# Output gates of an mLSTM cell as half of 1 + tanh(o/2), one block at a time, on one Trainium2 core

## The chip, the core and the metric

The kernel runs on one core of a Trainium2 chip. The core has five engines with an instruction queue each: TensorE (PE) for matmuls and transposes, VectorE (DVE) and ScalarE (ACT) for elementwise work, GpSimd (POOL), and SyncE (SP), which here only issues DMAs. Each engine works strictly in the order of its own queue, and waits for another engine or for a DMA by a semaphore. The metric is device time in microseconds (us); lower is better.

## What is computed

Two blocks, the second fed by the first.

The mLSTM cell has 4 batches, 8 heads, 768 positions and a head size of 40. For every position t (shortened from the reference):

```python
m_new  = max(f_gate[t] + m, i_gate[t])
f_stab = exp(f_gate[t] + m - m_new);  i_stab = exp(i_gate[t] - m_new)
C = f_stab * C + i_stab * outer(v[t], k[t])
n = f_stab * n + i_stab * k[t]
h_tilde = C @ q[t]
denom = max(abs(n . q[t]), 1)
o = 1 / (1 + exp(-o_gate[t]))          # the output gate
y[t] = o * h_tilde / denom
```

The result becomes 3072 rows of 320 numbers. Hash routing sends every row to one of 8 experts, `token_ids * 2654435761 % 8`, which is `token_ids % 8`; an expert is two matmuls, 320 to 1024 with a ReLU, and 1024 to 320. All data is float32.

## The kernel before, in words

**The two stages.** The first stage works in the chunked form of the cell: a block is 128 positions of one batch, all 8 heads. There are 24 blocks, and the loop `for s in range(NT)` handles one per step, batch by batch within a chunk of positions, so that the state of a batch is used again four steps later. The finished rows `x` go to a DRAM tensor, `x_rows`. The second stage gathers the rows of each expert from there by indirect DMAs (`gather`, line 109) and runs the experts one after the other.

**The order of the work** is written out by hand (`manual_schedule`): what a step calls, in which order, is the order on each engine's queue. For a step s this is, with the lines of the profile:

- SP: loads of the gate rows `R` for step s+3 (line 210), of k and q for s+5 and v for s+4 (199), of the output gates `og` (195), then the stores of finished rows (457), then pieces of the first expert's weights (130 to 136).
- `divided(s-1)` on DVE (446 to 450): the division of block s-1, which reads the PSUM tile `xh` of that block and writes `x`.
- `turn(s+2)`: transposes of k and q on PE (332), copied out of PSUM (333), as a rule by ACT.
- pieces of the routing, a few small DVE and POOL operations each, listed by step in `pieces`. `route_hot(0..7)` builds one-hot matrices for 3 blocks each (DVE 614 and 622, POOL 619); every second one is followed at the end of its step by `route_table` (PE 630, then DVE 633 and 635). `route_index` makes the row lists (DVE 640 to 653), `route_tiles` the list of extra tiles (DVE 554 to 562).
- `scores(s+1)` on PE (379), `k_weights(s+1)` on POOL (365), `decays(s+1)`: PE 343, two `exp` on ACT (347), PE 351, then `qs` on DVE (355) and `dec` on ACT (357).
- `gated(i)` on POOL (454): x times the output gate.
- `state(s)`: PE 410 into the PSUM tile `xh` of the next block, a copy `add` on ACT (414), two additions on POOL (420). There is none from step 20 on.
- `weigh(s+1)` on DVE (385), then `attend(s)` on PE (431, 437).

At step 21 the first two gathers of expert 0 are issued on POOL; they read the rows of blocks 0 to 19, so they wait for those stores. At steps 22 and 23 their results are transposed on PE (`early_turn`, 675), ahead of `attend(23)`.

**The output gates before.** They are loaded in three groups of 8 blocks into a tile of 2560 elements per partition (2 buffers), from step 3 to 6, 7 to 11 and 13 to 16. One sigmoid (371) works on a whole group, at the end of steps 7, 12 and 17. The sigmoid and the `exp` of `decays` need different function tables, so a table load stands before each sigmoid and another before the next `exp`. In the step after a sigmoid the two copies of `turn` go to DVE and no block is gated. In the others up to two blocks a step are gated, from step 9 on; the gating stands ahead of `state(s)` on POOL's queue. `x` has 10 buffers, as blocks wait for their gates.

Of the kernel before, what the change touches and what calls it, by code (L numbers as in the profile page):

```python
# [17 lines left out]
P = 128  # L18
# [4 lines left out]
def kernel(  # L23
# [127 lines left out]
    with tc.tile_pool(name="gates", bufs=1) as gp, \  # L151
# [6 lines left out]
        NG, KV, RB = 8, 6, 3  # L158
# [26 lines left out]
        def rows_of(src, s):  # L185
            b, c = place(s)
            return src[b, :, c * P : (c + 1) * P, :].rearrange("h p d -> p h d")

        def load(s, what, eng=None):
            d = st.setdefault(s, {})  # L190
            eng = eng or nc.sync
            if what == "o":
                if s % NG == 0:
                    og[s // NG] = ld.tile([P, NG, H, D], F32, name="og", bufs=2)
                eng.dma_start(og[s // NG][:, s % NG], rows_of(o_gate, s))
            else:
                bufs, src = {"k": (ks, k), "q": (qs, q), "v": (vs, v)}[what]
                d[what] = bufs[s % KV]
                eng.dma_start(d[what][:, :, :D], rows_of(src, s))
# [127 lines left out]
        def turn(s, what, on_act=True):  # L327
            d = st[s]
            d[what + "T"] = wk.tile([P, PR, P], F32, name=what + "T", bufs=3)
            tp = ps.tile([P, PR, P], F32, name="tr", tag="tr", bufs=2)  # L330
            for j in range(PR):
                nc.tensor.transpose(tp[:, j, :], d[what][:, 2 * j : 2 * j + 2, :].rearrange("p h d -> p (h d)"), ident[:])  # L332
            (nc.scalar.copy if on_act else nc.vector.tensor_copy)(d[what + "T"][:], tp[:])
# [36 lines left out]
        def sigmoid(g):  # L370
            nc.scalar.activation(og[g][:], og[g][:], AF.Sigmoid)  # L371
# [70 lines left out]
        def divided(s):  # L442
# [6 lines left out]
            d["x"] = wk.tile([P, H, D], F32, name="x", bufs=10)  # L449
            nc.vector.tensor_tensor(d["x"][:], hs[:, :, :D], den[:].to_broadcast([P, H, D]), op=ALU.mult)  # L450

        def gated(s):
            x = st[s]["x"]
            nc.gpsimd.tensor_tensor(x[:], x[:], og[s // NG][:, s % NG], op=ALU.mult)  # L454
# [182 lines left out]
        def route_index():  # L637
# [20 lines left out]
            21: [route_index], 22: [route_tiles],  # L658
        }
        products = {4: [route_turned], 5: [route_counts]}  # L660
        for i, j in enumerate((11, 12, 14, 15, 16, 17, 19, 20)):
            pieces.setdefault(j, []).append(lambda i=i: route_hot(i))
            if i % 2:
                products[j] = [lambda i=i // 2: route_table(i)]
        for i, part in enumerate(slices_of(0)):
            pieces.setdefault((17, 18, 19, 20, 21, 22, 23)[i], []).append(part)
        sig_at = {7: 0, 12: 1, 17: 2}
        o_at = {}
        for i, j in enumerate((3, 3, 4, 4, 5, 5, 6, 6, 7, 8, 8, 9, 9, 10, 10, 11, 13, 13, 14, 14, 15, 15, 16, 16)):
            o_at.setdefault(j, []).append(i)  # L670
# [60 lines left out]
        nsig, ndone, waiting = -1, 0, {}  # L731
        for s in range(NT):
# [15 lines left out]
            for i in o_at.get(s, ()):  # L748
                load(i, "o")
# [10 lines left out]
            if s + 2 < NT:  # L760
                if s > 0:
                    turn(s + 2, "k", s - 1 not in sig_at)
                    turn(s + 2, "q", s - 1 not in sig_at)
# [14 lines left out]
            for i in range(2):  # L778
                if ndone < s and ndone // NG <= nsig and s - 1 not in sig_at:
                    gated(ndone)  # L780
                    waiting.setdefault(s + 1, []).append(ndone)
                    ndone += 1
# [11 lines left out]
            if s in sig_at:  # L794
                nsig = sig_at[s]
                sigmoid(nsig)
# [24 lines left out]
        while ndone < NT:  # L821
            gated(ndone)
            waiting.setdefault(NT, []).append(ndone)
            ndone += 1
# [202 lines left out]
```

## Time and profile before

| | |
|---|---|
| median of 5 runs | 386.65 us (386.06 to 387.17) |
| the profiled execution: its time, its span | 387.15 us, 385.3 us |
| busy share of the span, PE / DVE / ACT / POOL | 95% / 35% / 29% / 37% |
| first stage, up to the first expert matmul (873) | 136.24 us |
| 20 to 120 us: ACT busy / DVE busy / POOL busy | 63.6 / 78.2 / 67.7 us of 100 |

The span runs from the program's first instruction to its last. Busy time is the time in which an engine worked on an instruction; PE's matmuls are pipelined, so its own share is not a share of its peak. In a timeline row the columns are start (us), duration (us), engine, line, operation, what it writes and reads, shapes, count, and in brackets the idle time just before it with the instruction that ended it. Rows of one kind that follow closely are merged (x2, x16). The PSUM tile written by PE 332 at the head of a step marks its start; such starts give the length of each step.

### The profile page before, as it was taken

The numbers are of one execution on the slowest core, as the hardware profiler recorded it, in microseconds if no ns is written. First come the engines' busy times: TensorE is split into PE (matmuls) and PEld (weight loads), VectorE is DVE, ScalarE is ACT, GpSimd is POOL, SyncE is SP. The second block draws the span as 40 slices with busy tenths as digits, with TensorE's granted clock in tenths as the row PEclk, the third lists the DMA queues.
The fourth block names the chain that finished last, engine by engine and source line by source line (L and its number), as shares of the span: only waits on it lengthen the run. The fifth ranks groups of instructions, "written<-read, shape, count | busy, mean of one in ns | idle before, by whom it ended". The sixth has DMA issues, their size and how long they took to land.

```text
span 385.3 us, 7944 instructions
## 1 busy us (share of the span) xinstructions
PE 366.9 (95%) x3213; PEld 256.2 (66%) x3213; DVE 136.2 (35%) x354; ACT 112.8 (29%) x232; POOL 142.3 (37%) x243
## 2 busy tenths in 40 slices
PE   8989999899999889999999999999999999999991
PEld 8778788788878766865655655565665665664560
DVE  7568686988878821212012012002102102101100
ACT  6565576485585311111011111111111111101100
POOL 8433466889977417240141150124023020020121
PEclk9999999999999999999999999999999999999998
DMA  7699999998998599281721720442362000000000
GB/s 149 118 169 167 181 163 179 217 182 168 189 252 215 171 302 351 97 284 57 256 94 43 260 97 19 153 161 66 109 199 68 1 34 17 0 35 18 0 27 25
DMA packets 123797, 51.02 MB, mean 132 GB/s; under 512 B 103723, under 2 KB 119751, under 8 KB 123759
## 3 DMA queue, kind: packets, MB, share of 16 engines
q1 hardware_dynamic: 116254, 36.73, 41.1%
q0 software_dynamic: 2496, 8.20, 6.5%
q10 hardware_dynamic: 5008, 5.57, 4.7%
q8 instruction: 26, 0.43, 0.5%
q14 instruction: 13, 0.10, 0.1%
HBM read 42.10 MB, written 8.71 MB: 132 GB/s over the span
## 4 chain that ended last, share of the span: by engine, by line
PE 65%; DVE 7%; DMA 7%; POOL 6%; issue 6%; ACT 5%; SPq 2%; POOLq 0%; ACTq 0%; DVEq 0%
PE zp L902 22%; PE mh L873 22%; PE mh L866 6%; DMA x_rows<-x 4%; PE tr L332 2%; PE sp L379 2%; POOL x L454 2%; DVE w L385 2%; PE un L681 2%; ACT og L371 2%; DMA xr<-x_rows,g_idx 2%; PE xh L437 2%; PE tp L849 1%; PE zp L943 1%; PE ab L343 1%
## 5 line engine op out<-in xcount | busy, mean ns | idle before, releaser
L902 PE MATMUL zp<-w2t,h 128*128 128x320 f32 x384 | 105.5, 433 | 0.0
L873 PE MATMUL mh<-xT,w1t 128*128 128x416 f32 (+2 forms) x288 | 97.0, 481 | 1.3 <-DVE x L450 1.3
L902 PEld LDWEIGHTS zp<-w2t,h 128*128 128x128 f32 x384 | 72.6, 190 | 31.5 <-issue 2.9
L873 PEld LDWEIGHTS mh<-xT,w1t 128*128 128x128 f32 x288 | 51.3, 190 | 39.8 <-issue 37.8
L836 POOL DMA_INDIRECT out_dram<-zo,s_idx x26 | 25.7, 989 | 88.6 <-ACT zo L835 88.3
L855 DVE COPY xT<-tp 128x384 f32<-128x384 f32 x15 | 8.4, 557 | 127.9 <-PE tp L851 127.9
L882 ACT ACTIVATE h<-mh 128x416 f32<-128x416 f32 (+2 forms) x36 | 17.2, 479 | 110.0 <-PE mh L866 59.4
L835 ACT COPY zo<-zp 128x320 f32<-128x320 f32 x26 | 11.1, 426 | 101.4 <-PE zp L902 93.1
L880 DVE TENSOR_SCALAR h<-mh 128x416 f32<-128x416 f32 (+2 forms) x36 | 19.5, 543 | 59.2 <-PE mh L866 31.5
L437 PE MATMUL xh<-v,w 128*64 128x41 f32 x768 | 34.6, 222 | 0.0
L385 DVE TENSOR_TENSOR w<-sp,w 128x512 f32<-128x512 f32 x48 | 30.8, 681 | 8.5 <-ACT w L347 8.5
L379 PE MATMUL sp<-qT,kT 64*128 64x128 f32 x384 | 29.7, 285 | 2.4 <-DVE w L385 2.1
L347 ACT ACTIVATE w<-ab 128x512 f32<-128x512 f32 x48 | 26.1, 596 | 17.0 <-PE ab L343 17.0
L974 POOL COPY hrem<-h 128x256 f32<-128x256 f32 x8 | 3.2, 400 | 74.3 <-ACT h L882 74.3
L437 PEld LDWEIGHTS xh<-v,w 128*64 128x64 f32 x768 | 30.6, 138 | 0.0
L109 POOL DMA_INDIRECT xg<-x_rows,g_idx x24 | 23.4, 974 | 15.9 <-PE mh L866 6.9
L379 PEld LDWEIGHTS sp<-qT,kT 64*128 64x128 f32 x384 | 24.6, 187 | 7.0 <-issue 2.8
L866 PE MATMUL mh<-xT,w1c 64*128 64x416 f32 (+2 forms) x144 | 27.9, 497 | 0.1
L431 PE MATMUL xh<-C,qs 128*64 128x82 f32 x320 | 27.3, 249 | 0.0
L420 POOL TENSOR_TENSOR C<-C,add 64x164 f32<-64x164 f32 x32 | 17.8, 557 | 17.3 <-ACT add L414 16.1
L454 POOL TENSOR_TENSOR x<-x,og 128x320 f32<-128x320 f32 x24 | 20.5, 871 | 6.7 <-DVE x L450 6.6
L365 POOL TENSOR_TENSOR kw<-k,kwT 128x320 f32<-128x320 f32 x20 | 14.4, 724 | 12.5 <-PE xh L410 8.2
(187 smaller groups left out, 385.9 us busy)
## 6 DMA issues: line engine op xcount, KB each, us to landing
w2t<-in_moe_w_dram SPq DMA_DIRECT2D x5, 1280.0 KB
w1t<-in_moe_w_dram SPq DMA_DIRECT2D x5, 1024.0 KB
k<-in_k_dram SPq DMA_DIRECT2D x24, 160.0 KB
v<-in_v_dram SPq DMA_DIRECT2D x24, 160.0 KB
og<-in_o_gate_dram SPq DMA_DIRECT2D x24, 160.0 KB
x_rows<-x SPq DMA_DIRECT2D x24, 160.0 KB
q<-in_q_dram SPq DMA_DIRECT2D x23, 160.0 KB
w2t<-in_moe_w_dram ACTq DMA_DIRECT2D x2, 1280.0 KB
```

The lines of the kernel that those rows point to most:

```text
L109: nc.gpsimd.indirect_dma_start(out=xg, out_offset=None, in_=x_d[:rows, :], in_offset=bass.IndirectOffsetOnAxis(ap=idx, axis=0),)
L347: nc.scalar.activation(w[:, hf], ab[:], AF.Exp)
L379: nc.tensor.matmul(sp[hf][:, j, :], lhsT=d["kT"][r, j, :], rhs=d["qT"][r, j, :], start=True, stop=True)
L385: nc.vector.tensor_tensor(d["w"][:, hf], d["sp"][hf][:], d["w"][:, hf], op=ALU.mult)
L431: nc.tensor.matmul(xh[t, 2 * j : 2 * j + 2, :], lhsT=d["qs"][:, j, t], rhs=Cs[b][c % 2][:, j].rearrange("p h d -> p (h d)"), start=True, s ...
L437: nc.tensor.matmul(hs[t, 2 * j + hf, :], lhsT=d["w"][:, hf, j, t], rhs=d["v"][:, 2 * j + hf, :], start=(c == 0), stop=True, skip_group_che ...
L454: nc.gpsimd.tensor_tensor(x[:], x[:], og[s // NG][:, s % NG], op=ALU.mult)
L836: ins = nc.gpsimd.indirect_dma_start(out=out[:, :], out_offset=bass.IndirectOffsetOnAxis(ap=idx, axis=0), in_=zo[:], in_offset=None, bound ...
L866: nc.tensor.matmul(hp[i][:, : c1 - c0], lhsT=w1c[r, fp, :], rhs=xT[r, 2, c0:c1], start=first, stop=not first,)
L873: nc.tensor.matmul(hp[i][:, : c1 - c0], lhsT=w1t[:, db, fb * P : (fb + 1) * P], rhs=xT[:, db, c0:c1], start=(first and db == 0), stop=(not ...
L880: nc.vector.tensor_relu(h[:, 2 * fp, c0:c1], hp[i][:, : c1 - c0])
L902: nc.tensor.matmul(zp[:], lhsT=h[:, fb, j * P : (j + 1) * P], rhs=w[2][:, fb, :], start=(fb == 0), stop=(fb == FB - 1),)
```

## The change

- Each block's output gates have their own tile of 320 elements per partition, 6 buffers. They are loaded two steps ahead of their use (at step 21 for step 23), after v's load in SP's queue as before.
- The gate is computed by two ACT operations on that tile: `tanh(o/2)`, then half of it plus 0.5. They stand after `state(s)`, ahead of `attend(s)`. In the built order of the changed kernel the only table load on ACT is the very first one.
- Blocks 0 to 7 get their gates at steps 4, 5, 5, 6, 7, 7, 8, 9, and block i from 8 on at step i+1, but 22 and 23 both at step 23. A block is gated on POOL right after its gate, so after `state(s)` and not ahead of it, and stored at the next step: the first store is at step 5 instead of 10.
- All copies of `turn` are on ACT. `x` has 8 buffers.
- `route_hot` runs at steps 11 to 18 (before: 11, 12, 14, 15, 16, 17, 19, 20), the tables at 12, 14, 16, 18 (before 12, 15, 17, 20), `route_index` at 20 (21), `route_tiles` at 21 (22).

```diff
@@ def load
-                if s % NG == 0:
-                    og[s // NG] = ld.tile([P, NG, H, D], F32, name="og", bufs=2)
-                eng.dma_start(og[s // NG][:, s % NG], rows_of(o_gate, s))
+                og[s] = ld.tile([P, H, D], F32, name="og", bufs=6)
+                eng.dma_start(og[s][:], rows_of(o_gate, s))
@@ def turn
-            (nc.scalar.copy if on_act else nc.vector.tensor_copy)(d[what + "T"][:], tp[:])
+            nc.scalar.copy(d[what + "T"][:], tp[:])
@@
-        def sigmoid(g):
-            nc.scalar.activation(og[g][:], og[g][:], AF.Sigmoid)
+        def gate(s):
+            nc.scalar.activation(og[s][:], og[s][:], AF.Tanh, scale=0.5)
+            nc.scalar.activation(og[s][:], og[s][:], AF.Copy, scale=0.5, bias=0.5)
@@ def divided
-            d["x"] = wk.tile([P, H, D], F32, name="x", bufs=10)
+            d["x"] = wk.tile([P, H, D], F32, name="x", bufs=8)
@@ def gated
-            nc.gpsimd.tensor_tensor(x[:], x[:], og[s // NG][:, s % NG], op=ALU.mult)
+            nc.gpsimd.tensor_tensor(x[:], x[:], og.pop(s)[:], op=ALU.mult)
@@ the plan by steps
-            21: [route_index], 22: [route_tiles],
+            20: [route_index], 21: [route_tiles],
-        for i, j in enumerate((11, 12, 14, 15, 16, 17, 19, 20)):
-            pieces.setdefault(j, []).append(lambda i=i: route_hot(i))
+        for i in range(8):
+            pieces.setdefault(11 + i, []).append(lambda i=i: route_hot(i))
             if i % 2:
-                products[j] = [lambda i=i // 2: route_table(i)]
+                products[11 + i] = [lambda i=i // 2: route_table(i)]
-        sig_at = {7: 0, 12: 1, 17: 2}
-        o_at = {}
-        for i, j in enumerate((3, 3, 4, 4, 5, 5, 6, 6, 7, 8, 8, 9, 9, 10, 10, 11, 13, 13, 14, 14, 15, 15, 16, 16)):
-            o_at.setdefault(j, []).append(i)
+        gates_of = {}
+        for i, j in enumerate((4, 5, 5, 6, 7, 7, 8, 9)):
+            gates_of.setdefault(j, []).append(i)
+        for i in range(8, NT):
+            gates_of.setdefault(min(i + 1, NT - 1), []).append(i)
@@ the loop
-            for i in o_at.get(s, ()):
+            for i in gates_of.get(s + 2, ()) if s + 2 < NT - 1 else gates_of[NT - 1] if s == NT - 3 else ():
                 load(i, "o")
...
-                    turn(s + 2, "k", s - 1 not in sig_at)
-                    turn(s + 2, "q", s - 1 not in sig_at)
+                    turn(s + 2, "k")
+                    turn(s + 2, "q")
...
-            for i in range(2):
-                if ndone < s and ndone // NG <= nsig and s - 1 not in sig_at:
-                    gated(ndone)
-                    waiting.setdefault(s + 1, []).append(ndone)
-                    ndone += 1
             state(s)
...
-            if s in sig_at:
-                nsig = sig_at[s]
-                sigmoid(nsig)
+            for i in gates_of.get(s, ()):
+                gate(i)
+                if i < s:
+                    gated(i)
+                    waiting.setdefault(s + 1, []).append(i)
             if s == NT - 1:
                 early_turn(1)
             attend(s)
```

## The prediction

> **What bounds the kernel now.** I read the page's slices first, then PE's waits in the first stage, then the timeline step by step. From 136 us on PE works without a break on the experts and the change touches nothing there: what it is worth is decided before 136 us.
>
> ```profile
> PE   8989999899999889999999999999999999999991
> ...
> DMA  7699999998998599281721720442362000000000
> ```
>
> One slice is 9.6 us. PE is near full in the first 14 slices too, and so are the DMA queues; ACT is busy 63.6 of the 100 us from 20 to 120. So I measure steps by PE's starts of the k transposes: steps 7 and 8 take 4.83 us each (49.36, 54.19, 59.02), with no gap; a `route_table` adds 0.27 on PE, and 0.25 in the next step, where the q transposes wait for the copy out of PSUM. 4.83 plus these is the floor, and gains can come only from steps above it. PE's waits from 16 to 136 us (total us, times, longest) name them:
>
> ```profile
> PE xh L410 <- POOL C L390: 1.3, 1, 1.3
> PE sp L379 <- DVE w L385: 1.3, 2, 0.9
> PE tr L332 <- ACT dec L357: 0.9, 2, 0.4
> PE tr L332 <- ACT kT L333: 0.7, 1, 0.7
> ...
> PE tk L630 <- POOL oh_c L619: 0.2, 1, 0.2
> ```
>
> The two waits for `dec` belong to sigmoids. ACT's groups (count, busy us, mean ns) give the durations:
>
> ```profile
> L835 ACT COPY zo<-zp 128x320 f32<-128x320 f32 x26 | 11.1, 426 | 101.4 <-PE zp L902 93.1 <-PE zp L943 8.2
> L371 ACT ACTIVATE og<-og 128x2560 f32<-128x2560 f32 x3 | 7.0, 2339 | 0.0
> ...
> L371 ACT ACT_TABLE_LOAD x3 | 3.8, 1283 | 1.0 <-DMA x_rows<-x 1.0
> L347 ACT ACT_TABLE_LOAD x3 | 3.8, 1283 | 0.1
> ```
>
> **Part 1, the sigmoids go.** Each holds ACT for 1.28 + 2.34 + 1.28 = 4.9 us, 14.7 in all. What PE loses is in the rows after the first and the third:
>
> ```profile
> 60.10 0.66 PE L332 MATMUL tr<-ident,q 128*128 128x128 f32 x4 [0.43 <-ACT dec L357]
> ...
> 112.83 0.66 PE L332 MATMUL tr<-ident,q 128*128 128x128 f32 x4 [0.44 <-ACT dec L357]
> ```
>
> Step 9 runs from 59.02 to 64.68, 5.66 us, and step 19 from 111.74 to 117.41, 5.67: 0.83 and 0.84 over 4.83, the wait and the slower matmuls after it. The second sigmoid costs nothing: step 13 is 5.11 = 4.83 + 0.25 and step 14 is 4.83. Gain 1.67. The Trainium skill, "ScalarE: Activation LUTs", section "What ACT_TABLE_LOAD costs", counts about 2.66 us for a switch, a load of 1283 ns and a drain of 1380. The load agrees to the nanosecond, but here the `exp` starts at 111.64, 0.01 us after its load ended: no drain is paid, and by the rule the same sum would credit 16 us of ACT time instead of 7.7, still only as PE sees it.
>
> **Part 2, the gates come.** The trace has no tanh and no ACT copy of 128x320 within SBUF. Below, the nearest row is the copy above, 0.426; above, a line through an `exp` of 128x128 (0.312) and the sigmoid of 2560 (0.834 ns an element) gives 0.472 for 320. A pair, the second waiting for the first, is 0.85 to 0.94; I take 0.94, as its operands are in SBUF like the upper rows'. 24 pairs are 22.6 us, and the six copies of `turn` return to ACT from DVE (6 x 0.59 = 3.5): ACT is busier by 11. The cover: after `add` ACT idles until the next k transposes are done, 1.35 us in a full step ("1.35 <-PE tr"). A single pair fits. At steps 5, 7 and 9 two pairs, 1.9, end 0.55 late; the 0.80 that ACT then waits for `ab` takes it up, except at step 6, whose q transposes already wait 0.7 for `kT`: ACT idles 1.5 before it, so 1.9 costs 0.35 (0 to 0.55). Were the cover gone (a pair above 2.1), each step would pay the excess one for one. DVE loses six copies of 0.68; it is not late in those steps, so nothing. A rule against this: the same page, "Rules for kernel authors", gives multiplications and additions to VectorE, not ScalarE. By it the second half of a gate would leave ACT, 24 x 0.47 = 11 us, and join DVE, which is busy 16.2 of the 20 us from 100 to 120; no run here shows that form.
>
> **Part 3, step 11.** It lasts 6.37 (69.51 to 75.88), 1.54 over. The wait is put down to C L390, but PE 410 writes the PSUM tile that `x` L450 reads until 73.68, and 410 starts at 73.78. That `x` is late because DVE works on `e_zt` (lines 311, 312, 302, 303) from 69.48 to 72.38, two of the four at 0.83 against 0.66 for the first while POOL gates two blocks beside them, and because its buffer's store is not down (0.29). With stores from step 5 on, block 10's buffer is long free: 0.29 goes; POOL gates one block there, later: 0.3 of the slow operations may go. I take 0.6; bounds 0 and 1.54. At step 12 PE waits 0.22 for `oh_c`, as POOL is late by two gatings; with one gating a step (0.87 less) I take 0.25 (0 to 0.38).
>
> **Part 4, POOL, SP, DMA.** POOL runs the same 24 gatings of 0.87, now behind `state`. A step with `route_hot` has 0.73 + 0.9 + 0.72 + 1.08 + 0.87 = 4.3 us of it, under 4.83; `kw` is needed 3 us later than it ends. Step 10 adds 2.9 for the slots; POOL then runs 3 us late, and nothing waits for that before step 12's end. SP issues the same 24 loads and 24 stores. A load lands about 2.7 us after its issue (49.31 to 52.65 for one `og`). At the crowded end SP starts step s about 3.4 us after PE does, so `og` lands some 10.5 us into step s and is used 14 us in: 3.5 us spare. Cost 0; what it costs if that is gone is the rival below.
>
> **Part 5, the end of the stage.**
>
> ```profile
> 123.80 0.86 POOL L454 TENSOR_TENSOR x<-x,og 128x320 f32<-128x320 f32 x1 [1.72 <-DVE x L450]
> ...
> 126.99 0.16 ACT L357 COPY dec<-xb 128x4 f32<-128x4 f32 x1 [1.01 <-DVE qs L355]
> 127.03 1.19 POOL L109 DMA_INDIRECT xg<-x_rows,g_idx  x1 [2.36 <-DVE qs L355]
> ...
> 132.63 0.66 PE L675 MATMUL tpx<-ident,xg 128*128 128x128 f32 x4 [0.65 <-DVE xg L805]
> ```
>
> Now the first gather waits for the store of block 19, down at 126.10. In the changed kernel a new wait stands ahead of it on POOL: `gated(20)` waits for its gate, which stands behind `dec` of block 22 on ACT, and that behind `qs` on DVE. From the start of step 20: `route_index` (about 2.1 without POOL beside it) ends at 3.4, `weigh` at 5.3, step 21's division at 6.5, `route_tiles` at 7.65, `qs` 8.35, `dec` 8.55, gate 9.55, gating 10.45, first gather 10.75. Before it is 127.03 - 117.41 = 9.62, so 1.1 later, and 1.65 with the 0.52 by which a table moved ahead of step 20. The second gather lands 3 us after its issue, at 15.3; `attend(23)` starts at 15.8, or 16.3 with the 0.52; before, 133.22 - 117.41 = 15.8. Cost 0.5. PE itself gets there 0.6 sooner than before, so the lower end is -0.6; the upper is the gather's 1.65.
>
> **Sum**: -0.83 - 0.84 - 0.60 - 0.25 + 0.35 + 0.50 = -1.67 us. On the profiled execution, 387.15 us (span 385.3, 1.85 around it), that is 385.5. The median of the runs shown, 386.65, lies 0.5 below it, so I forecast 385.0.
>
> **Rivals.** 0.2%, 0.77 us, is about what a measurement of this kernel can tell from no change.
> - *Forecast*, 384 to 386 by halves of the terms: 0.45.
> - *The end eats it.* Step 11 keeps its 1.54 and the gather costs its full 1.65: -1.67 - 0.25 + 0.35 + 1.65 = +0.1, 386.7. For it: the new wait is certain. Against: DVE has slack there. 0.22.
> - *More goes.* Step 11 and 12 fall to the floor and the end gains: -1.67 - 1.54 - 0.38 - 0.6 = -4.2, 382.5. 0.15.
> - *Slower: ACT waits for `og` at steps 19 to 21.* Loads of `og` now share steps 18 to 21 with the expert's weights, whose slices take 1.6 to 3.3 us of the queue. From the point where `og` lands over 3.5 us later than worked out, every us holds `kT` and the next `exp` behind the gate. 1.2 a step over three steps, 3.6 - 1.67 = +1.9: 388.6. Against: before, the same steps carried two stores a step, and SP's lateness did not grow. 0.13.
> - *It doesn't do what it says*, tanh being slower than its bounds: up to 1.35 a pair it is covered, so 386.2. 0.05.
>
> Faster by over 0.2%: 0.41 of the forecast, the 0.15 and 0.01, so 0.57; slower: 0.13 and 0.03 of the end's case, 0.16; the rest, 0.27, within. The range takes in all bounds, -4.2 to (-1.67 + 0.55 + 1.65) = +0.5: 382.5 to 387.2, leaving out the slower rival.
>
> **What would show it.** Right: one table load on ACT, steps 9 and 19 at 4.83 to 5.1 with no wait for `dec`; PE's wait before 675 or its gather later by about a us; step 6 longer by 0.3. Wrong: ACT idle before a gate until an `og` DMA lands; a step above 5.5 from 13 to 19; or a division so late on DVE that 410 waits in other steps.

## The result

| | before | after |
|---|---|---|
| median | 386.87 us (56 runs) | 389.43 us (30 runs) |
| ratio, 95% interval | | 1.0057 (1.0043 to 1.0072) |
| the profiled execution: its time, its span | 387.15, 385.3 | 390.59, 388.8 |
| its mean granted clock | 0.997 | 0.981 |
| first expert matmul starts | 136.24 | 137.87 |

The change made the kernel slower by 0.57%, some 2.2 us (the two medians differ by 2.56). The forecast was a gain of 1.67 us. Of the page of after, these are the rows of slices (one is 9.7 us) for PE, for the granted clock and for DMA:

```profile
PE   7989899999999789999999999999999999999991
...
PEclk9999999999999779999999999999999999999997
DMA  7699998998997589363632631452272000000000
```

New against before, from the second slice on, is a 7 on PE in slice 14 and, there and in the next, a 7 in the clock, which had been 9 up to the last slice. The clock records of the trace say it exactly: 0.5 of full speed from 131.44 us for 10.24 us, then 1.0 again. PE's waits from 16 to 136 us (total, times, longest) name what came just before it:

```profile
PE tpx L676 <- DMA xg<-x_rows,g_idx: 2.9, 1, 2.9
PE tr L331 <- ACT kT L332: 1.5, 2, 0.8
PE tr L331 <- ACT dec L356: 0.5, 1, 0.5
...
PE sp L379 <- DVE w L385: 0.4, 1, 0.4
```

Four of the five waits shown of before have shrunk or gone (410 no longer waits for POOL, nor `tk` for `oh_c`; `dec` 0.5 for 0.9; `w` 0.4 for 1.3), and the one for `kT` has grown from 0.7 to 1.5. One that was not there stands above them: 2.9 us for the first gathered rows. ACT's groups (count, busy us, mean ns) show the change itself as it was costed:

```profile
L370 ACT ACTIVATE og<-og 128x320 f32<-128x320 f32 x24 | 11.4, 477 | 0.0
L371 ACT ACTIVATE og<-og 128x320 f32<-128x320 f32 x24 | 11.3, 471 | 0.8
...
L261 ACT ACT_TABLE_LOAD x1 | 1.3, 1283 | 1.7 <-PEq L1007 1.7
```

**Step by step.** By the transposes of k, as in the prediction:

| step | 5 | 6 | 9 | 11 | 12 | 13 | 14 | 19 |
|---|---|---|---|---|---|---|---|---|
| before | 5.24 | 5.66 | 5.66 | 6.37 | 5.51 | 5.11 | 4.83 | 5.67 |
| after | 5.90 | 5.77 | 4.83 | 4.83 | 6.16 | 5.30 | 5.10 | 5.11 |

Step 20 starts at 116.36 instead of 117.41, and the scores of block 23 at 125.15 instead of 127.65: the first stage's compute is 2.5 us faster. Then all of it is lost, and more. The chain of work that ended last, from the store of block 19 on (start, us, what):

```profile
123.08 3.45 DMA x_rows<-x
...
126.68 0.86 issue
127.54 4.34 DMA xg<-x_rows,g_idx
131.88 0.14 issue
132.02 1.51 PE tpx L676 x6
```

No compute stands in it between 123.08 and 132.02: a store, the issue of the gather on POOL, the gather. PE gets its rows at 132.0, `attend(23)` starts at 133.46 (before 133.22), and from there the half clock costs 3.2 us: `attend(23)` and the wait behind it last 4.41 instead of 3.02, and the first layer of the first expert 12.11 instead of 10.28. In all -1.05 to the start of step 20, +1.3 to `attend(23)` (0.64 of it are the six transposes of gathered rows at half clock, 1.51 us for the 0.87 that they take in the trace of e8), +3.2 behind it: +3.45, the 390.59 - 387.15 of the two profiled executions. Over all timed runs of after, the time follows the mean clock: 390.1 to 391.0 at 0.981 or 0.982 (13 runs), 389.2 to 389.7 at 0.985, 387.7 to 389.4 at 0.989 or 0.990, and 386.3 to 387.4 at 0.993 and above (4 runs). These four are no slower than before, but it isn't known whether their gathers were also early.

### The profile page after: what moved, and what is told of

Read it like the earlier page. It is cut to its first block, busy times and chain, and to the rows that moved or that the text cites. A ratio compares the mean times of both kernels' runs of the same rounds, so it can differ in the third digit from the quotient of the medians.

```text
span 388.8 us, 7989 instructions
## 1 busy us (share of the span) xinstructions
PE 368.8 (95%) x3213; PEld 258.0 (66%) x3213; DVE 133.5 (34%) x348; ACT 121.1 (31%) x277; POOL 142.5 (37%) x243
## 2 busy tenths in 40 slices
DMA packets 123796, 51.02 MB, mean 131 GB/s; under 512 B 103722, under 2 KB 119750, under 8 KB 123758
## 4 chain that ended last, share of the span: by engine, by line
PE 81%; DVE 6%; issue 5%; ACT 2%; DMA 2%; POOL 1%; POOLq 0%; SPq 0%; ACTq 0%; DVEq 0%
PE mh L869 24%; PE zp L898 23%; PE mh L862 7%; PE sp L379 6%; PE tr L331 5%; PE xh L437 4%; PE xh L431 3%; PE ab L342 3%; PE xh L410 2%; PE tp L845 1%; PE zp L939 1%; DMA xg<-x_rows,g_idx 1%; PE xb L350 1%; DVE w L385 1%; POOL out_dram L832 1%
## 5 line engine op out<-in xcount | busy, mean ns | idle before, releaser
L869 PE MATMUL mh<-xT,w1t 128*128 128x416 f32 (+2 forms) x288 | 98.8, 488 | 1.4 <-DVE x L450 1.4
L869 PEld LDWEIGHTS mh<-xT,w1t 128*128 128x128 f32 x288 | 52.4, 194 | 40.3 <-issue 37.9
L437 PE MATMUL xh<-v,w 128*64 128x41 f32 x768 | 35.5, 226 | 0.0
L437 PEld LDWEIGHTS xh<-v,w 128*64 128x64 f32 x768 | 31.4, 141 | 0.0
L420 POOL TENSOR_TENSOR C<-C,add 64x164 f32<-64x164 f32 x32 | 16.2, 508 | 14.8 <-ACT add L414 13.5
```

Of the source, the lines that this page charges most:

```text
L437: nc.tensor.matmul(hs[t, 2 * j + hf, :], lhsT=d["w"][:, hf, j, t], rhs=d["v"][:, 2 * j + hf, :], start=(c == 0), stop=True, skip_group_che ...
L869: nc.tensor.matmul(hp[i][:, : c1 - c0], lhsT=w1t[:, db, fb * P : (fb + 1) * P], rhs=xT[:, db, c0:c1], start=(first and db == 0), stop=(not ...
```

## The experiments

Ratios are to runs of the kernel before on the same chip, with their 95% intervals. Each diff is against the changed kernel, if nothing else is said.

### PE kept busy

```diff
+                unread(10)     # e11_warm_6: unread(6)
                 early_turn(0)
```

> The changed kernel with ten matmuls of the identity (`unread(10)`, nobody reads them, 0.265 us each at full clock by the 1.06 us of the `un` row of 8 records) on PE between attend(22) and early_turn(0), where PE idled 2.90 us in the changed kernel. Theory A (the clock): the loss is the granted clock, 0.5 from 131.44 for 10.24 us, which follows from PE's idle time; with PE busy until about 131.8 the clock stays at 1.0, the gathers land at the same 132, and the time falls by the 3.2 us that the slow clock cost: 386.2 to 387.0, the same as before. Rival B (the wait): the later gather is the loss and the clock is an accident; the gather lands no earlier, so nothing changes: about 389.4. Rival C (the cost sits in the gates on ACT): also 389.4.

> The changed kernel with six unread matmuls (1.6 us) instead of ten ahead of early_turn(0). The ten kept PE until 132.2 in a trace in which the second gather was down at 131.57, so they held up PE by 0.6 us themselves. Theory A: a gap of 1.3 us or less is left, the clock stays 1.0, and the time is that of before within 0.5 us (0 to +0.15%). Rival B: half the clock comes back at random, 388 to 389.

Ten: 387.47 us, 1.0024 (1.0005 to 1.0042). Six: 388.52, 1.0025 (1.0007 to 1.0044). With ten the mean clock was 0.993 to 0.997 in all 12 runs; with six in 9 of 12. In the trace with ten it is 1.0 until 380.34 us. So PE's idle time does close the clock, and theory A has that part right: the excess falls from 0.57% to 0.25%, by about 1.2 us. It is wrong that nothing is left. The other 1.0 us isn't the clock, and the trace with ten shows where 0.65 of it arises. Its experts start at 135.85, 0.39 us sooner than in before, and its store of block 23 goes out at 136.74 instead of 137.07. But that store takes longer, and the rows `xr`, gathered behind it, are later (chain of before; chain with ten; then PE's rows of both for `xr`):

```profile
137.07 6.01 DMA x_rows<-x
```

```profile
136.74 6.60 DMA x_rows<-x
...
145.45 6.53 DMA xr<-x_rows,g_idx
```

```profile
151.84 0.41 PE L849 MATMUL tp<-ident,xr 128*128 128x128 f32 x2 [0.53 <-DMA xr<-x_rows,g_idx]
```

```profile
152.16 0.41 PE L846 MATMUL tp<-ident,xr 128*128 128x128 f32 x2 [0.35 <-DMA xr<-x_rows,g_idx]
```

The first expert's second output block starts at 152.90 instead of 152.25, 0.65 us later, and from there to the end all three traces (before, after, ten matmuls) take the same 233.1 us. So in these kernels the time of a run is decided when that block starts, and PE waits for `xr` ahead of it in before too: coming there sooner wins nothing unless the transfers come sooner as well. With six, the profiled run is one of those in which the first gather went out late (128.91) and PE idled another 2.25 us behind the six matmuls; there the clock closed again.

### PE given real work: attend(23) first

```diff
+            attend(s)
             if s == NT - 1:
+                for j in range(2): nc.vector.tensor_copy(xg0[:, j, Dm:], xg0[:, j, 2 * P : Dm])
+                early_turn(0)
                 early_turn(1)
-            attend(s)
```

(with the copies and `early_turn(0)` taken out of step 22)

> The changed kernel with the last attend(23) on PE ahead of the two transposes of gathered rows instead of behind them (and DVE's copies of gathered rows behind the division of block 22). PE's 2.90 us of waiting are then filled with the 2.2 to 3.0 us of attend(23). Theory A: no gap over about 1 us is left, the clock stays 1.0, attend(23) runs from 129.2 to 131.4, the transposes from 132.0 to 133.4, DVE's division of block 23 runs beside them, and the experts start at about 134.1 instead of 137.87 (136.24 before): the first stage's 2.5 us come through, about 384.5 to 385. Rival B (the gather is the bound and whatever PE does ahead of it is hidden anyway, the start of the experts being held by the later gathers that need the last stores): 386.5 or more. Rival C (gates on ACT): 389.

384.81 us, 0.9974 (0.9942 to 1.0007). Eight of the 12 runs took 383.9 to 385.4, at a clock of 0.993 to 0.997; the other four 387.2 to 389.5, at 0.988. In the trace, one of the four, PE got the rows at once, but then waited 1.34 us for their copies to `xT0`, which stood on ACT behind the gate of block 23, and the clock was 0.5 from 133.95 for 3.41 us. In the eight runs in which the clock stayed open, 0.5% faster than before by their middle, what the first stage won seems to come through.

The same edit on the kernel before:

> The kernel before with attend(23) ahead of the transposes of gathered rows, and nothing of the change. Theory A (the end of the stage held back whatever the change won, and the change is worth about 2 us once it does not): PE comes to attend(23) 2.5 us later than with the change, the experts start at about 135.5, `xr` is no longer waited for: 385.0 to 385.6, 1 us slower than the changed kernel with the same edit. Rival E (the change wins nothing even so, all comes from the new order): 384.0 to 384.5, as fast as with the change or faster.

385.69 us, 0.9958 (0.9936 to 0.9981), the clock 0.993 to 0.997 in all runs. The kernel before gains 0.4% from it too: its end was held by transfers as well. By their ratios, 0.9974 and 0.9958, the two kernels with `attend(23)` first can't be told apart, so this pair doesn't show that the change is worth anything, and rival E isn't excluded by it.

### One part of the change alone

The diffs put back, in the changed kernel, the steps of `route_hot`, `route_index` and `route_tiles` of before (e3), or make only that move in the kernel before (e4).

> The changed gates with the routing steps of before (one-hot pieces at 11, 12, 14 to 17, 19, 20; index at 21, tiles at 22). Theory A: steps 9 and 19 fall by 0.83 and 0.84 without the routing's help, step 5/6 costs the 0.78 it cost in the changed kernel, step 11 falls as there, so PE comes to the gather about 1.5 to 2.5 us earlier than before and waits 2.2 to 3.1 us: on the edge of where the clock closes. Either it stays open and the time is that of before, 386.5 to 387.2, or it closes and it is 389 to 390. Rival D (the routing move makes the gather late, the gates are innocent): the gather is issued 0.5 us sooner after step 20 begins, and the time is 385.2.

> The kernel before with the routing steps of the change alone (one-hot pieces in steps 11 to 18, index at 20, tiles at 21; the sigmoids stay). Theory A: steps 9 and 19 keep their stalls, PE comes to the gather at most 0.5 us earlier than before, waits about a us, and the clock stays 1.0: 386.4 to 387.2. Rival D (the routing move carries the loss): 388.5 to 389.5.

Gates alone: 388.01 us, 1.0039 (1.0017 to 1.0061). Routing alone: 387.65, 1.0030 (1.0008 to 1.0051), at a clock of 0.993 and above. So rival D, in which one part is innocent, falls; but theory A missed that the routing move costs 0.3% with the clock open. Its first gather is issued early (125.67) and its experts start at 135.92; what is late in its trace is the last link, the rows `xr` at 152.12. Why the median is 1 us more than that of the kernel before on that chip stays open (in the trace the second output block starts 0.35 us later than in before, 152.60). The trace meant to show it,

> The kernel before, word for word, once more, for a trace from the chip on which the other experiments run: 386.3 by the median of its 35 runs beside the first four experiments. Every theory expects the same; what is to be read is the last link: when the store of block 23 is issued, when it is down, and when PE gets the rows of `xr` (151.84 in the first trace).

took 390.76 us. Its clock was 0.5 for 3.41 us from 115.14, in the middle of the first stage, after PE had waited 1.52 us for `dec` behind the third sigmoid (0.44 in the first trace). It tells only that the kernel before is not free of this either, and that the stall behind a sigmoid varies.

### The clock closed on purpose, in the kernel before

```diff
+                dm = wk.tile([P, H, D], F32, name="dm", bufs=1)
+                nc.gpsimd.memset(dm[:], 0.0)
+                for _ in range(2):
+                    nc.gpsimd.tensor_tensor(dm[:], dm[:], dm[:], op=ALU.mult)
                 for j in range(2):
                     gather(xg0[:, j, :Dm], g_idx[:, j : j + 1], TE * P)
```

> The kernel before with a memset and two multiplications of 128x320 on POOL ahead of the first gather, on a tile that nobody reads: the gathers are issued some 2.3 us later. Theory A: PE idles about 3 us ahead of the transposes, as in the changed kernel, and the clock closes: 2.3 + 3.2 us more, 391 to 392. Rival B (PE's idle time costs only itself): 388.0 to 388.7, clock 1.0.

389.95 us, 1.0058 (1.0029 to 1.0086). The clock was 0.5 from 131.80 in the trace, and the mean clock 0.986 to 0.992 in nine of ten runs (in one of 29 runs of the kernel before on that chip). But PE's wait isn't where it was meant to be. The first gather goes out at 127.94, 0.9 us later than in the first trace, and the transposes of its rows don't wait; PE waits ahead of the scores of block 23:

```profile
130.04 1.73 PE L379 MATMUL sp<-qT,kT 64*128 64x128 f32 x16 [2.24 <-DVE w L385]
```

DVE is late there because three operations of `route_index` took 1.35 us longer beside the new POOL work (lines 641, 647 and 649: 1.16, 0.71 and 0.70 us, for 0.86, 0.18 and 0.18 in before). So a wait of PE is followed by a closed clock in the kernel before as well, as theory A says; where the wait came from, and the size, are not as forecast: the clock was closed for one stretch of 3.41 us instead of three.

### The last link: the store of block 23, the gather behind it, and the weights

First the gates of blocks 22 and 23 in step 22, so that nothing stands ahead of the copies to `xT0`:

```diff
-            gates_of.setdefault(min(i + 1, NT - 1), []).append(i)
+            gates_of.setdefault(min(i + 1, NT - 2), []).append(i)
```

(their loads and gatings follow; `attend(23)` first)

> The changed kernel with attend(23) first, and the gates of blocks 22 and 23 in step 22 in place of step 23 (the trace with attend(23) first shows the gate of block 23 on ACT from 131.80 to 132.96, between the transposes of the gathered rows and their copies to xT0, and PE waiting 1.34 us for these copies; then the granted clock is 0.5 from 133.95). Theory A (PE's idle time closes the clock): PE waits under 0.8 us, the clock stays at 1.0 in all runs, 383.3 to 384.3. Rival B (the clock falls by chance, whatever PE waits): the two values of the last kernel again, some runs at 384, some at 387 to 389. Rival C (the gate was covered): no change, 384.8.

388.87 us, 1.0036 (1.0010 to 1.0063): slower, which no theory had. PE's rows:

```profile
133.24 1.99 PE L871 MATMUL mh<-xT,w1t 128*128 128x256 f32 x8 [0.91 <-ACT xT L677]
...
151.10 0.44 PE L847 MATMUL tp<-ident,xg 128*128 128x128 f32 x2 [3.85 <-DMA xg<-x_rows,g_idx]
```

The experts start at 133.24, 3 us sooner than before the change, and then PE waits 3.85 us for the third tile of gathered rows. The rows on SP and POOL (the stores of blocks 22 and 23; the gather that needs them) tell why:

```profile
131.71 6.27 SPq L457 DMA_DIRECT2D x_rows<-x  x2
```

```profile
144.60 0.98 POOL L109 DMA_INDIRECT xg<-x_rows,g_idx  x1 [10.60 <-DMA w2t<-in_moe_w_dram]
```

With its gates done, ACT issued the next expert's weights from 131.23 on, and the stores went into the queues beside them: block 23 was gated at 133.99, and its store went out at 137.65, 3.7 us later. That is a third link, behind the first gather and `attend(23)`: store of block 23, gather, `xr`. Two kernels have these weights behind the first output blocks instead:

```diff
-                layer1(W[0], xT0, h, 0, 2 * P, lambda fp: len(W) < 3 and load_weights(len(W), nc.scalar))
+                layer1(W[0], xT0, h, 0, 2 * P)
...
+                    load_weights(1 + j, nc.scalar)     # after output block j
```

> The changed kernel with attend(23) first, and the loads of the second and third expert's weights (2 x 2.56 MB on ACT's queue) issued behind the first and second output block of the first expert instead of within its first layer. In the trace with the gates of 22 and 23 moved, these loads are issued from 131.23, SP's stores of blocks 22 and 23 then take 6.27 us to be issued, the gather that needs them is issued at 144.60 and PE waits 3.85 us for its rows at 151.10. Theory F (the store of block 23 and the gather behind it are the last link of the end, and the weights on the DMA queues stretch it): the store is down 3 us after its issue, the gather is issued by 140, PE doesn't wait, the experts go from 133.2 to the second output block at 148.7 in place of 152.3: 383.0 to 384.0. Rival G (the link is long whatever else is on the queues): 384.8 to 387.

> The changed kernel with attend(23) first, gates 22 and 23 in step 22, and the late weights. Theory F: the gates in step 22 were not what made that kernel slow (388.87), but the weights that ACT then issued 2 us sooner, ahead of the last stores; with the weights late it is as fast as the kernel with attend(23) first and late weights alone, or up to 0.5 us faster: 382.6 to 384. Rival H (three gates in step 22 hold up ACT or the og loads): 386 or more.

With `attend(23)` first and late weights: 386.56 us, 0.9957 (0.9931 to 0.9982). With gates 22 and 23 moved too: 387.47, 0.9978 (0.9951 to 1.0005), against 1.0036 without late weights. So theory F holds for the kernel that had been slow, by its trace: the gather behind the last store is issued at 138.9 instead of 144.6, and PE doesn't wait for `xr`'s transfer. By their times alone both would fit the rivals G and H: they took longer than forecast, by 2.6 and 3.5 us. Two reasons show in the traces. From the second output block to the end they take 233.8 us instead of 233.1, as do all five traces with late weights. And in both the first gather went out at 129.46, and with it came PE's wait and the clock (0.5 for 6.83 us):

```profile
132.70 0.41 PE L676 MATMUL tpx<-ident,xg 128*128 128x128 f32 x2 [1.64 <-DMA xg<-x_rows,g_idx]
...
135.44 3.78 PE L868 MATMUL mh<-xT,w1t 128*128 128x256 f32 x8 [0.57 <-ACT xT L677]
```

The 3.78 is the row to know a closed clock by: the same eight matmuls take 1.97 to 1.99 in the others.

The same two edits on the kernel before:

> The same two edits on the kernel before, without the change. Theory F: the link is loosened here too; in the kernel before with attend(23) first PE started the experts at 133.8 and the second output block at 150.1, a wait of some 0.8 us among it, which goes: 384.0 to 385.0. What the change is worth once nothing at the end holds it is the difference to the last kernel: 0.5 to 1.5 us. Rival E (the change is worth nothing or less even then): 383.5 or less, as fast as the changed kernel or faster.

386.74 us, 0.9989 (0.9968 to 1.0010). The forecast was 384.0 to 385.0; the late weights gave it nothing over `attend(23)` first alone (0.9958).

### What makes the first gather late

In the traces so far with the changed gates and the changed routing steps, the rows of block 19 are gated at 122.3 to 122.4. Its store was issued by SP at 122.4 to 124.6, was down at 124.4 to 128.4, and the gather followed about a us later, or 0.2 us after `gated(20)`, whichever was last: 126.6 to 129.5. Most of this varies without any edit: after, e1, e2, e9, e11 and e18 are the same program up to there, and in their traces the store goes out at 123.08, 122.41, 122.41, 124.58, 124.39 and 124.08. First suspect all the same, the og loads that SP now issues in steps 18 to 21:

```diff
-                og[s] = ld.tile([P, H, D], F32, name="og", bufs=6)
+                og[s] = ld.tile([P, H, D], F32, name="og", bufs=10)
...
+                o_at.setdefault(j - 2 if i < 14 else 13 + (i - 14) // 2, []).append(i)
```

> The changed kernel with the og loads of blocks 14 to 23 in steps 13 to 17, two a step (ten buffers instead of six), so that SP has none in steps 18 to 21; nothing else differs. Theory S (SP's lateness: og loads and weight slices hold the store of block 19 behind them on SP): that store is issued at 122.4, as soon as its block is gated, is down by 124.6 to 125, the first gather is issued at 126.6, when POOL is through with gated(20), and PE idles 2.0 to 2.2 us instead of up to 2.9. The clock closes less often, not never, so the time falls by half: +0.1 to +0.35% over before. Rival T (the queues are late by chance, whatever SP issues): the store is again issued anywhere from 122.4 to 124.6, and the time is +0.55%. Rival U (loads in steps 13 to 17 crowd k, q and v of these steps): steps 14 to 18 longer than in the changed kernel, later than +0.55%.

389.14 us, 1.0039 (1.0010 to 1.0069). Theory S isn't borne out by the trace: with no og load in steps 18 to 21, the store of block 19 is still late. The time can't tell theory S from rival T, as its interval takes in both forecasts (SP; then POOL):

```profile
122.50 0.34 SPq L457 DMA_DIRECT2D x_rows<-x  x1
123.78 0.38 SPq L136 DMA_DIRECT2D w2t<-in_moe_w_dram  x1
124.26 0.42 SPq L457 DMA_DIRECT2D x_rows<-x  x1
```

```profile
128.79 1.20 POOL L109 DMA_INDIRECT xg<-x_rows,g_idx  x1 [2.32 <-DMA x_rows<-x]
```

The first row is the store of block 18, itself issued 4.7 us after its gating ended (117.79). SP is late all along, and the queues are busy nearly all the time. The stretches 100 to 126 and 126 to 136 us of before and of after (busy us of PE, PEld, DVE, ACT and POOL, then granted clock, DMA share, GB/s):

```profile
100.00:126.00 26.00, 25.31 (x482) 21.57 (x480) 21.47 (x56) 16.63 (x31) 19.69 (x32) 1.00 0.91 216
126.00:136.00 10.00, 7.24 (x150) 6.01 (x146) 8.30 (x27) 2.27 (x6) 3.90 (x4) 1.00 0.56 171
```

```profile
100.00:126.00 26.00, 25.62 (x484) 21.86 (x482) 21.00 (x63) 17.50 (x41) 14.40 (x23) 1.00 0.93 207
126.00:136.00 10.00, 7.10 (x118) 6.28 (x116) 3.81 (x11) 4.60 (x11) 4.31 (x5) 0.77 0.54 162
```

The DMA share is 0.91 and 0.93 up to 126 us, and 0.92 to 1.00 from 20 to 100. Both kernels move 51.02 MB. The change takes nothing off that; it only lets PE reach the end of it sooner. The test takes the first expert's weights out of the store's way:

```diff
-            pieces.setdefault(17 + i, []).append(part)
+            pieces.setdefault((21, 21, 21, 22, 22, 23, 23)[i], []).append(part)
```

> The changed kernel with the seven slices of the first expert's weights in steps 21, 21, 21, 22, 22, 23, 23 instead of 17 to 23: none of their 2.56 MB is issued ahead of the store of block 19, where 1.6 MB were. Theory D (the stage is paced by its DMA traffic, share 0.93 from 100 to 126 us, and PE's 2.5 us do not make that traffic shorter): with 1.6 MB less, some 7 us at the 207 GB/s of that stretch, SP is not late, the store of block 19 goes out at 122.4, within 0.3 of its gating, is down by 124.8, and the first gather is issued at 126.6, behind gated(20). What the time does is open: the weights now share the queues with the gathers and the last stores, so PE's wait may be as long as before and the time +0.3 to +1%. Rival T (chance): the store goes out at 123 to 124.6 as in four of the traces.

393.08 us, 1.0107 (1.0072 to 1.0142). The store is as theory D has it (SP; then POOL, gating of block 20 and gather):

```profile
122.38 0.34 SPq L457 DMA_DIRECT2D x_rows<-x  x1
```

```profile
125.56 0.86 POOL L454 TENSOR_TENSOR x<-x,og 128x320 f32<-128x320 f32 x1 [3.20 <-ACT og L371]
126.59 1.20 POOL L109 DMA_INDIRECT xg<-x_rows,g_idx  x1 [0.17 <-issue]
```

It is down at 124.18, and the gather waits for `gated(20)` alone. The time got worse, since the gathers and the last stores now share the queues with the weights (PE waits 2.24 and 0.71 us for gathered rows, and the clock is 0.5 for 10.24 us). It is one trace; the store also went out at 122.41 in the traces of e1 and e2, with the weights ahead of it. That traffic paces the store is thus supported, by the share and by this run, and not settled for each run.

### The end set free

```diff
+            if s == NT - 3:                 # moved ahead of gated(20) on POOL
+                for j in range(2):
+                    gather(xg0[:, j, :Dm], g_idx[:, j : j + 1], TE * P)
             for i in gates_of.get(s, ()):
                 gate(i)
```

This with `attend(23)` first and early og loads is e16; with late weights too, e14; with the first gates in steps 6 to 11 in addition, e15; and with `attend(23)` first alone, e18.

> The changed kernel with all that the runs pointed to at its end: og loads in steps 13 to 17, the first two gathers on POOL ahead of gated(20), attend(23) ahead of the transposes of gathered rows, and the next experts' weights behind the first output blocks. The first gather goes out about a us after the store of block 19 is down, 125.6 to 126, PE has attend(23) until 131.2 and then no wait over 0.7, so the clock stays 1.0 and the second output block starts at 148.2: 382.8 to 383.8, -0.75 to -1.0%, with few runs above 385. Rival E (the change wins nothing even with the end free): no faster than the kernel before with the same order of attend(23) and late weights, -0.1%.

> The same, with the first gates in steps 6 to 11 (6, 7, 7, 8, 8, 9, 9, 10, 10, 11, 11) instead of 4 to 9. In the changed kernel the gate of step 4 makes kT late and step 5 lasts 6.29 us instead of 5.62, step 6 lasts 5.95 instead of 5.85. If the gates are the cause, these 0.78 us come back (5.62 and 5.85) and the time is 0.5 to 0.8 us below the last kernel's; if two gates in each of steps 7 to 11 cost as much elsewhere, it is the same.

> As the kernel with the end free, but with the weights of the next experts where the changed kernel has them. Theory F: PE starts the experts as early (133), the store of block 23 and the gather behind it are again stretched to 11 us or more, PE waits 1 to 4 us for these rows, and the time is 1 to 3 us above that of the kernel with late weights. Rival G: the same time.

> The changed kernel with two edits alone: attend(23) on PE ahead of the transposes of gathered rows, and the first two gathers on POOL ahead of gated(20). The og loads in steps 13 to 17 did nothing by themselves, and the late weights nothing that shows between the kernels with and without them, so these two should do what all did: 384.0 to 385.0, -0.6 to -0.9% by ratio, the clock at 1.0 in most runs. If the og loads matter together with them: -0.3%, as with attend(23) first alone.

| | median | ratio |
|---|---|---|
| e14, all | 384.69 | 0.9934 (0.9910 to 0.9958) |
| e15, and later first gates | 384.09 | 0.9917 (0.9887 to 0.9947) |
| e16, without late weights | 384.69 | 0.9920 (0.9897 to 0.9943) |
| e18, without early og loads too | 390.75 | 1.0063 (1.0037 to 1.0088) |

e15 beats both kernels: the one before by 0.83%, the changed one by the two ratios by 1.4%. e14, forecast at 382.8 to 383.8, took 0.9 us more than that, but it is 0.55% ahead of the kernel before with `attend(23)` first and late weights (0.9989), so its rival E falls. Against the best order tried for the kernel before, `attend(23)` first alone (0.9958), e15 is ahead by 0.4%, and the two intervals overlap a little; the kernel before wasn't given the other edits. So the first stage's gain probably comes through once PE has work while the rows travel; how much of it is the change's, and how much the new order's, isn't settled. e16 is as fast as e14: theory F had 1 to 3 us more for it, so rival G holds, and the late weights give nothing here either. In e15's trace, the clock is 1.0 to 377.5 us and PE goes from the scores to the experts with one wait over 0.3 us (the experts start 3.2 us before those of the kernel before):

```profile
133.05 1.97 PE L873 MATMUL mh<-xT,w1t 128*128 128x256 f32 x8 [0.85 <-DVE x L450]
```

Its steps 5 and 6 are 5.23 and 5.67, as before the change (the figures in its forecast count steps from the starts of the scores), so the 0.77 us did come with the early gates; but step 12 is then 7.30 instead of 6.16, and step 20 starts at 116.51, no sooner. What it is faster by over e14 is within the intervals.

e18 missed its forecast, 384.0 to 385.0, by some 6 us. It differs from e16 in the og loads alone, and by 1.4% by the ratios: what showed nothing in e13 seems to decide here. That isn't shown, since e16 and e18 ran on different chips and the store of block 19 varies without any edit. In the trace of e18 the store of block 19 goes out at 124.08, the gather at 128.57; the gatings of blocks 20 to 22 now stand behind it on POOL, so their stores leave from 131.94 on, into the weights, the last of them at 138.63, and the third tile of rows is late:

```profile
152.70 0.44 PE L844 MATMUL tp<-ident,xg 128*128 128x128 f32 x2 [3.87 <-DMA xg<-x_rows,g_idx]
```

In e16 these four stores leave from 129.37 to 133.33. A late gather ahead of the gatings only moves the wait from the first link to the third.

## Why the prediction was wrong, point by point

**The sum against the traces.** Without the 0.50 of the end, the terms add up to -2.17 at the start of step 20; measured -1.05 (some 0.55 of the difference are pieces of a table that the prediction counts in Part 5). From there to `attend(23)` the sum has +0.50; measured +1.3. Behind `attend(23)` it has nothing; measured +3.2. The end and what lies behind it are the step that failed.

**Part 1, the sigmoids: right in these two traces.** Step 9 fell by 0.83, to 4.83, one table load is left, and `dec` holds nothing there. Step 19 fell by 0.56 instead of 0.84, as some 0.27 of a table now falls into it. Another 0.27 falls into step 14; the prediction has these two as 0.52, in Part 5. The size is that of one trace: in e7, e8 and e10, which keep the sigmoids and the routing steps of before, step 9 takes 5.95 to 6.17 and step 19 4.83 to 6.57.

**Part 2, the gates: the duration right, the cost from elsewhere.** A pair measures 0.48 + 0.47 and takes 0.98 from start to end, against 0.94. The 0.35 was put at step 6, as ACT's lateness behind two pairs. That came to 0.11; and step 5 lost 0.66 (ACT, then PE, from 37 to 40 us):

```profile
37.34 0.48 ACT L370 ACTIVATE og<-og 128x320 f32<-128x320 f32 x1
37.85 0.47 ACT L371 ACTIVATE og<-og 128x320 f32<-128x320 f32 x1
39.15 0.58 ACT L332 COPY kT<-tr 128x512 f32<-128x512 f32 x1 [0.83 <-PE tr L331]
```

```profile
39.79 0.66 PE L331 MATMUL tr<-ident,q 128*128 128x128 f32 x4 [0.68 <-ACT kT L332]
```

By the ACT rows the gate of step 4 is covered: ACT then idles 0.83 until the transposes of k are done. What the q transposes wait for is the copy of the k tile of their own step, over at 39.73, as if both were in the same one of the two PSUM buffers. In the program before, the q tile of this step seems to have the other buffer, that of `tpe` (512), read by DVE at 38.91, and starts at 39.13, while `kT` is still being copied. So the 0.66 isn't ACT's time but, as far as these waits tell, a buffer assignment that came out differently with the new order; no run sets it by itself. In e15, with other gate steps, q starts at 39.10 again, and steps 5 and 6 are back.

**Part 3, steps 11 and 12: the sum right, by another split.** Step 11 lost its whole stall, 1.54, and not 0.60. Step 12 got 0.65 longer instead of 0.25 shorter, and step 13 0.19 longer: DVE's late work now holds `qs`, `dec` and the transposes of q one step on (0.48 us of wait at 75.42). Together -0.70, against -0.85.

**Part 4, POOL, SP and DMA at nothing: right for the og loads, not for SP.** The og loads were in time and no gate waited for one, so the slower rival, ACT waiting for og at steps 19 to 21, did not happen. It named the right queue and steps and the wrong victim: what SP's lateness holds is the store of block 19. In the profiled run it goes out 0.75 us after its gating (123.08 - 122.33), behind two og loads; in e9 it is 2.2 us, in e1 and e2 it is nothing. (The row that the prediction gives for a load that lands 2.7 us after its issue, 49.31 to 52.65, is 3.3 us from the start of the issue.)

**Part 5, the end: the step that failed.** "Cost 0.5" counted the gather from the start of step 20, as if it moved with the compute, and let the gain ahead of it through to the experts. Measured from there, the first gather is issued at +11.2 (10.75 worked out, 11.27 with the table's 0.52), the second is down at +15.95 (15.3, or 15.8), and `attend(23)` starts at +17.1 (15.8 to 16.3), 1.3 later than before and not 0.5. The issue of the gather is thus as worked out; mis-sized are the second gather's landing, taken as 3 us after its issue (3.61 in before, 128.52 to 132.13, and 3.28 after), and the transposes behind it, 0.64 longer by the half clock. In the profiled run `gated(20)`, named as the limit, was over at 126.41; the store of block 19, down at 126.53, was the limit, and POOL issued a us later. `gated(20)` is the limit where the store is early (e1, e2, e17). So the end followed the transfers, and the 2.5 us that PE won became PE's wait (2.90 us ahead of the transposes, for 0.65 in before). The page had said so: the row of DMA slices was quoted in the first fence with 9s up to slice 12 and named in the text, and no term of the sum came from it.

**"From 136 us on PE works without a break": wrong in before too.** Its list of waits past 136 us has 0.5 us for `xr`, at 151.84. This was the sign of the third link, which took 3.85 us in e6 and 3.87 in e18. It is also why a gain ahead of 136 us could not reach the end by itself: with the clock held open (e1), the experts start 0.39 us sooner and the second output block still 0.65 us later.

**Not in the prediction at all: the clock.** It stood at 1.0 in every row of before, so no term or rival had it. By the runs with ten matmuls it is 1.2 us of the 2.2, and by the rows 3.2 us in the profiled run, 3.8 with the transposes; a loss of some 1.0 is left without it. The Trainium skill, "TensorE: Matmul & The Clock Gate", "Part 1: The HAM clock gate", says that a gate passes half or all of the clock, by PE's activity in windows of 4096 cycles, some 3.4 us, that run on their own. The runs agree in the lengths: closed stretches of 3.41, 6.83 and 10.24 us, and nothing but 0.5 and 1.0. The rule in that page's section "Why this matters for your kernels", no idle gaps over about 3 us, was no shelter here: the gap was 2.9 us, and the clock closed 2.3 us into it (131.44); in the kernel with the gates alone the clock closed at 132.73, after a wait of 1.85 us for the rows that had ended at 131.23.

**What stays open**: why the routing move alone costs 0.3% with the clock open, and what decides, run by run, whether SP is 0 or 2 us late; how much of the gain of e14 to e16 is the change's; and why e18 is 1.4% behind e16.

## What to carry to other kernels

Before crediting a saved stall, ask whether the next thing that the engine needs moves with it: here the rows came by a store and a gather that did not move with PE (beside a DMA share of 0.93), so PE's 2.5 us became a wait. A wait on PE costs more than itself when the clock closes behind it; fill it with work that is ready (`attend(23)` first gave 0.4% even to the kernel before). And a transfer late in a stage is to be followed to the end of its chain, past the first wait that it causes.

## What the runs showed of the hardware

- The granted clock closed during or after PE waits of 1.3 to 3.9 us, not in every run (a wait of 1.61 us at 74 us in e10 left it open), and, ahead of the kernel's last microseconds, each time for a multiple of 3.41 us. Eight matmuls that take 1.97 us then take 3.64 to 3.78.
- A store of 160 KB was down 1.8 us after its issue on quiet queues (124.18 - 122.38) and 6 to 8.5 us beside the loads of an expert's weights (140.15 - 131.64 in e16). There a store went out up to 3.7 us after its rows were ready (e6).
- The rows of the first two gathers were down 2.9 to 5.4 us after their issue (5.4 beside weights, in e17). For the gathers of the third tile and `xr` it was 2.9 to 7.9.
- Small DVE operations took 0.71 us instead of 0.18 beside POOL's multiplications (e8, line 647).
- After the one table load at its start ACT went between tanh, copies with scale and bias, and `exp` without another load.
